# Scores of the next round moved into the visit of updates, values and reads: a recurrence and FFN kernel with a rewritten start

## The chip, the cores and the metric

The kernel runs on one core of a Trainium2 chip. The metric is the device time of one execution in microseconds (us); the time of a version is the median of several executions. PE is TensorE (its weight loads are listed apart, as PEld), DVE is VectorE, ACT is ScalarE, POOL is GpSimd, and SP is the engine whose queue issues all the DMAs here.

## The reference, cut to what matters

A linear recurrence with decay (4 batches, 8 heads, 768 positions, head size 32, state size 16) is followed by a feed-forward layer on its output (3072 tokens, 256 to 2048 to 256, softplus between).

```python
log_a = np.log(np.clip(a, 1e-06, 1.0))
for c in range(nc):                                  # chunks of 32 positions
    cum = np.cumsum(la, axis=-1)
    L = np.exp(cum[:, :, :, None] - cum[:, :, None, :]) * causal
    M = np.einsum('bhin,bhjn->bhij', Cc, Bc) * L
    y_intra = np.einsum('bhij,bhjd->bhid', M, xc)
    y_inter = np.einsum('bhin,bhnd->bhid', Cc, state) * np.exp(cum)[..., None]
    y[:, :, sl] = y_intra + y_inter
    state = decay_full * state + np.sum(Bx, axis=2)
h = x @ w_in                                         # x is y, by token
out = (np.maximum(h, 0.0) + np.log1p(np.exp(-np.abs(h)))) @ w_out
```

## The kernel before, in words

The 768 positions are cut into 6 rounds u of 128. A round of the recurrence gives the 512 tokens (4 batches x 128 positions) on which the feed-forward layer then works as block j = u.

In the recurrence a round has two halves p (two batches each). For each half the **scores** (word `S u.p`, tiles sp0 to sp3, line 379) are 16 matmuls that contract only 32 rows, four at a time side by side on a quarter of PE's rows. POOL makes the **decays** (`D`, tile rm, line 352) with a masked select from the factors fc; DVE **weighs** the scores with them (`M`, line 394). Then come the **updates** of the state (`U`, tile zp), the **values** (`I`, tiles yp) and the **reads** of the old state (`R`, also yp), all small matmuls on parts of PE; DVE makes the next state (`N`), multiplies the values by the growth factors (`G`), and the sum is split into a high and a low part (`Xh` on ACT, `Xl` on DVE).

The feed-forward layer is done in 128 x 512 matmuls. For each of 16 slices k of the 2048 inner columns there are 6 matmuls hp (`F`: high and low parts, lines 586 to 606), the softplus and its split on ACT and DVE (`P`, tiles e, gh, gl), and 6 matmuls acc (`Z`, lines 626 to 661). The weights come as 64-bit numbers in sixteen pieces (`w`), and are split into high and low parts in six stages each on ACT and DVE (`W`, line 543).

At the start logs of the decays are taken (`loga`, `logr`) and summed by matmuls with triangular **sum matrices** kc that are made on chip (line 162), which gives the factors by token (`ft`: tiles fp and total, then exp) and by row (`fr`: tiles sums and rp, then exp). Before that a few matmuls on zeros (`warm`) keep PE busy.

Three things set the order. Up to step 42 all engines follow a list of words written out by hand (ORDER, line 58), and PE follows the written order everywhere. After ORDER a step s runs one `Z` and one `F` (12 big matmuls), and the words of a round u from 3 on are put in at steps counted from the round's begin (FILLS, line 85); the other engines' instructions are then placed by a scheduler. And every tile in PSUM that is not an accumulator comes from a ring of 6 banks (tag ps): scores take 4 of them, a visit's zp and yp take 3, each hp takes 1.

```python
FILLS = (
    (-16, "D@.0 un@+.0 un@+.1 gg@+"),
    (-11, "S@.0 M@.0.0 M@.0.1 M@.0.2 M@.0.3 D@.1"),
    (-9, "C@ B@.0 B@.1 T@"),
    (-8, "S@.1 M@.1.0 M@.1.1 M@.1.2 M@.1.3"),
    (-5, "U@ I@.0 I@.1 R@ G@.0 G@.1 Xh@.0 Xh@.1 Xl@.0 Xl@.1 N@"),
)
```

In the profile most instructions have line 131 (135 in the changed kernel): it is the helper that puts an operation into the written order. They are told apart by their tiles. In what follows a *visit* is a stretch in which PE leaves the 128 x 512 matmuls for small ones and comes back.

Of the kernel before, what the change touches and what calls it, by code (L numbers as in the profile page):

```python
# [21 lines left out]
P = 128  # L22
# [17 lines left out]
TOKEN_GROUPS = ((0, 3), (3, 6))  # L40
ROW_GROUPS = ((1, 3), (3, 6))
# [11 lines left out]
C_MID = C_OWN + 3 * NB * (NC + 1)  # L53
# [30 lines left out]
RM = 2  # L84
FILLS = (
    (-16, "D@.0 un@+.0 un@+.1 gg@+"),
    (-11, "S@.0 M@.0.0 M@.0.1 M@.0.2 M@.0.3 D@.1"),
    (-9, "C@ B@.0 B@.1 T@"),
    (-8, "S@.1 M@.1.0 M@.1.1 M@.1.2 M@.1.3"),
    (-5, "U@ I@.0 I@.1 R@ G@.0 G@.1 Xh@.0 Xh@.1 Xl@.0 Xl@.1 N@"),  # L90
)

def constants():
# [7 lines left out]
    unit = np.arange(3 * NB * (NC + 1)) // (NC + 1)  # L101
# [9 lines left out]
def recurrence_then_ffn(ctx: ExitStack, tc: tile.TileContext, un, alr, w_in, w_out, const, outT):  # L111
# [31 lines left out]
    NL = S * NB * NH // P  # L143
    NR = NB * NH
# [705 lines left out]
```

## Time and profile before

| what | value |
|---|---|
| time, median of 3 runs | 315.08 us (314.93 to 315.32) |
| the profiled execution: its own time | 316.49 us |
| its span, first to last instruction | 314.8 us |
| mean granted TensorE clock | 0.999 |
| PE busy | 310.1 us (99%), 2315 matmuls |
| PE weight loads busy | 253.5 us (81%) |
| DVE / ACT / POOL busy | 158.3 / 169.0 / 38.0 us |
| HBM read, written | 20.76 MB, 3.24 MB |

The profiled execution took 1.41 us longer than the median of the timed runs. Matmuls overlap in the records (one starts while the one before it drains), so that a busy PE is read by the distance between starts and not by the length of a matmul. "x32" in a row stands for 32 instructions in a row that are alike.

### The profile page before, as it was taken

What the parts mean: (1) busy time and instruction counts of PE and PEld (TensorE: products, weight loads), DVE (VectorE), ACT (ScalarE), POOL (GpSimd) and SP (SyncE); (2) the same over time, 40 slices, a digit from 0 to 9 for tenths busy, and PEclk for the clock granted to TensorE, in tenths of its full rate; (3) what the DMA queues carried; (4) which work ended last, traced back from release to release, by engine and by line L of the source; (5) the groups of instructions that cost most, each with busy time, mean ns of one, the idle gap of its engine ahead of it and who ended that gap; (6) DMA issues with size and microseconds to landing.
All of it is one profiled execution on the core that took longest, in us unless ns stands there. A gap on an engine that the chain in (4) does not pass through costs nothing.

```text
span 314.8 us, 5625 instructions
## 1 busy us (share of the span) xinstructions
PE 310.1 (99%) x2315; PEld 253.5 (81%) x2315; DVE 158.3 (50%) x254; ACT 169.0 (54%) x290; POOL 38.0 (12%) x47
## 2 busy tenths in 40 slices
PE   8999999999999999999999999999999999999995
PEld 5887788888888878888888888888888888888885
DVE  3989995635744553454933254552344342322222
ACT  5789899788636364343344534344534344634450
POOL 5760900000000500000600000500000000000000
PEclk9999999999999999999999999999999999999999
DMA  7956956504000351000520100000100000100001
GB/s 242 401 216 207 374 188 159 175 1 167 2 0 0 117 199 55 34 3 0 202 70 0 67 2 0 3 2 0 67 3 0 3 0 0 69 0 0 2 0 67
DMA packets 10298, 24.37 MB, mean 77 GB/s; under 512 B 1056, under 2 KB 1696, under 8 KB 10272
## 3 DMA queue, kind: packets, MB, share of 16 engines
q1 hardware_dynamic: 10272, 24.01, 22.1%
q8 instruction: 18, 0.29, 0.4%
q14 instruction: 8, 0.07, 0.1%
HBM read 20.76 MB, written 3.24 MB: 76 GB/s over the span
## 4 chain that ended last, share of the span: by engine, by line
PE 98%; issue 0%; DVE 0%; POOL 0%; DVEq 0%; POOLq 0%
PE hp L131 42%; PE acc L131 41%; PE yp L131 5%; PE sp L131 5%; PE warm L131 1%; PE gp L131 1%; PE fp L131 1%; PE end L131 1%; PE zp L131 1%; DVE rm L131 0%; PE total L131 0%; PE rp L131 0%; DVE o_end L131 0%; PE sums L131 0%; POOL some L131 0%
## 5 line engine op out<-in xcount | busy, mean ns | idle before, releaser
L617 DVE TENSOR_TENSOR gl<-e,gh 128x512 fp32r<-128x512 f32 x54 | 37.3, 692 | 88.7 <-ACT gh L614 88.7
L131 PE MATMUL hp<-xh,wih 128*128 128x512 f32 (+1 forms) x196 | 76.2, 389 | 0.2 <-DVE rm L131 0.2
L131 PE MATMUL hp<-xl,wih 128*128 128x512 f32 (+1 forms) x196 | 75.6, 386 | 0.0
L131 PE MATMUL hp<-xh,wil 128*128 128x512 f32 (+1 forms) x196 | 75.5, 385 | 0.0
L131 PE MATMUL acc<-gh,woh 128*128 128x512 f32 x188 | 74.4, 396 | 0.0
L611 ACT ACTIVATE e<-hp 128x512 f32<-128x512 f32 x54 | 32.3, 598 | 76.8 <-PE hp L131 76.5
L131 PE MATMUL acc<-gl,woh 128*128 128x512 f32 x188 | 73.5, 391 | 0.0
L131 PE MATMUL acc<-gh,wol 128*128 128x512 f32 x188 | 73.2, 389 | 0.0
L131 DVE TENSOR_TENSOR gl<-e,gh 128x512 fp32r<-128x512 f32 x42 | 29.3, 707 | 33.2 <-ACT gh L131 33.1
L131 PEld LDWEIGHTS hp<-xh,wih 128*128 128x128 f32 x196 | 36.8, 188 | 8.6 <-DVE rm L131 1.1
L131 PEld LDWEIGHTS hp<-xh,wil 128*128 128x128 f32 x196 | 36.8, 188 | 7.7 <-DVE wil L131 0.4
L131 PEld LDWEIGHTS hp<-xl,wih 128*128 128x128 f32 x196 | 36.8, 188 | 7.2
L131 PEld LDWEIGHTS acc<-gh,woh 128*128 128x128 f32 x188 | 35.3, 188 | 8.6 <-issue 0.9
L131 PEld LDWEIGHTS acc<-gh,wol 128*128 128x128 f32 x188 | 35.3, 188 | 7.4
L131 PEld LDWEIGHTS acc<-gl,woh 128*128 128x128 f32 x188 | 35.3, 188 | 7.4 <-DVE gl L131 0.3
L131 ACT ACTIVATE e<-hp 128x512 f32<-128x512 f32 x42 | 24.5, 594 | 23.5 <-PE hp L131 19.7
L614 ACT CAST gh<-e 128x512 fp32r<-128x512 f32 x54 | 33.5, 620 | 4.1 <-PE acc L131 2.4
L131 POOL TENSOR_SCALAR_AFFINE_SELECT rm<-fc 128x512 f32<-128x512 f32 (+1 forms) x26 | 24.7, 985 | 81.1 <-PE yp L131 77.4
L131 ACT CAST gh<-e 128x512 fp32r<-128x512 f32 x42 | 25.3, 616 | 10.8 <-PE acc L131 10.4
L131 ACT ACTIVATE signs<-wraw 128x512 f16<-128x512 f32 (+1 forms) x32 | 24.2, 782 | 0.0
L131 DVE TENSOR_TENSOR rm<-sp,rm 128x512 f32<-128x512 f32 x32 | 20.4, 682 | 7.1 <-PE sp L131 6.8
L356 POOL TENSOR_SCALAR_AFFINE_SELECT rm<-fc 128x2048 f32<-128x2048 f32 x4 | 10.5, 2641 | 84.4 <-PE yp L131 84.4
(93 smaller groups left out, 219.7 us busy)
## 6 DMA issues: line engine op xcount, KB each, us to landing
un<-in_un SPq DMA_DIRECT2D x10, 768.0 KB, 6.2
wraw<-in_w_in SPq DMA_DIRECT2D x8, 512.0 KB, 5.1
wraw<-in_w_out SPq DMA_DIRECT2D x8, 512.0 KB, 4.3
gg<-gd SPq DMA_DIRECT2D x20, 128.0 KB, 3.5
out_t<-o SPq DMA_DIRECT2D x9, 256.0 KB, 2.1
head_in_h<-in_un SPq DMA_DIRECT2D x2, 384.0 KB, 5.1
head_in_l<-in_un SPq DMA_DIRECT2D x2, 384.0 KB, 6.7
out_t<-half SPq DMA_DIRECT2D x2, 256.0 KB, 2.2
```

Of the source, the lines that this page charges most:

```text
L131: return lambda *a, **k: tc.keep_in_program_order(f(*a, **k))
L356: Pl.affine_select(out=weights_of(u, p)[:, ks].rearrange("p h (c i) -> p (h c) i", i=SUB), in_=fs.rearrange("p h c -> p (h c)").unsqueeze( ...
L611: A.activation(e, h, AF.Softplus)
L614: A.copy(gh, e)
L617: V.tensor_tensor(gl, e, gh.bitcast(F32), op=ALU.subtract)
```

## The change

The scores of a round's first half leave their own visit and stand behind the reads of the round before (`S@+.0` in the line of FILLS at -5; `S3.0` behind `R2` in ORDER); the scores of the second half keep a visit of their own. To have the decays that early, `D` of the first half is moved up by about a round, and for rounds 3 and 5 its tiles lie in the room of the raw weights (AHEAD_OF_TIME), in two pieces each. The logs come in two DMAs, first those of rounds 0 and 5 with the copy for the growth, then the others, and both groups of factors are cut accordingly. The sum matrices come from one select on POOL and seven small DVE operations. The zeros that `warm` writes are one tile, and there are eight such matmuls ahead of the first useful one and two further on. One half of the values of round 0 is put into an accumulator's bank. Two memsets go from DVE to POOL. ORDER is another list; of its 300 or so words the diff shows the first row only.

```diff
-TOKEN_GROUPS = ((0, 3), (3, 6))
-ROW_GROUPS = ((1, 3), (3, 6))
+NR = NB * NH
+LAST = NU - 1
+ROW_GROUPS = ((1, LAST), (LAST, NU))
...
-C_MID = C_OWN + 3 * NB * (NC + 1)
+C_MID = C_OWN + (LAST - 1) * NB * (NC + 1)
...
-la warm7 loga loga ft0 logr us0.0 w0 logr gb ft0 kb S0.0 ux0.0 W0 growth gq0 us0.1 growth ux0.1 D0.0.0 W0 M0.0.0 ft0 D0.0.1
...
+la warm6 warm1 kb loga lb warm1 loga logr logb fr1 fr1 logr us0.0 growth ft0 gb ft0 ft0 w0 ft0 ft0 D0.0.2 growth S0.0
...
+AHEAD_OF_TIME = ((3, 0), (5, 0))
 FILLS = (
-    (-16, "D@.0 un@+.0 un@+.1 gg@+"),
-    (-11, "S@.0 M@.0.0 M@.0.1 M@.0.2 M@.0.3 D@.1"),
+    (-16, "D@.1 un@+.0 un@+.1 gg@+"),
+    (-14, "D@+.0"),
+    (-11, "S@.1 M@.1.0 M@.1.1 M@.1.2 M@.1.3"),
     (-9, "C@ B@.0 B@.1 T@"),
-    (-8, "S@.1 M@.1.0 M@.1.1 M@.1.2 M@.1.3"),
-    (-5, "U@ I@.0 I@.1 R@ G@.0 G@.1 Xh@.0 Xh@.1 Xl@.0 Xl@.1 N@"),
+    (-5, "U@ I@.0 I@.1 R@ S@+.0 G@.0 G@.1 N@ Xh@.0 Xh@.1 Xl@.0 Xl@.1"),
+    (-4, "M@+.0.0 M@+.0.1 M@+.0.2 M@+.0.3"),
 )
...
-    both_logs = cp.tile([P, NA + NR + NL], F32, name="both_logs")
-    la, lr = both_logs[:, : NA + NR], both_logs[:, NA + NR :]
+    first_logs = cp.tile([P, 3 * NR], F32, name="first_logs")
+    other_logs = cp.tile([P, NA - 2 * NR + NL], F32, name="other_logs")
+    lo, lr = other_logs[:, : NA - 2 * NR], other_logs[:, NA - 2 * NR :]
-    level = cp.tile([P, 2], F32, name="level")
+    level = cp.tile([P, 1], F32, name="level")
...
-        Pl.memset(level[:, :1], 1.0)
-        Pl.memset(level[:, 1:], 0.5)
-        V.memset(kc, 0.0)
-
-        def below(rows, at, n, value, fill):
-            Pl.affine_select(
-                out=kc[rows, at : at + n],
-                in_=value[rows].broadcast_to([rows.stop - rows.start, n]),
-                pattern=[[-1, n]],
-                compare_op=ALU.is_gt,
-                fill=fill,
-                base=rows.start,
-                channel_multiplier=1,
-            )
-
+        Pl.memset(level, 1.0)
+        V.memset(kc[:, : NC * P], 0.0)
+        later = kc[:, NC * P :]
+        Pl.affine_select(
+            out=later,
+            in_=level.broadcast_to([P, P]),
+            pattern=[[-1, P]],
+            compare_op=ALU.is_gt,
+            fill=0.0,
+            base=0,
+            channel_multiplier=1,
+        )
         for c in range(NC):
             n = SUB * (c + 1)
+            own = slice(SUB * c, n)
             if c:
-                below(slice(0, SUB * c), c * P, n, level[:, :1], 0.0)
-            below(slice(SUB * c, n), c * P, n, level[:, 1:], -0.5)
-        below(slice(0, P), NC * P, P, level[:, :1], 0.0)
+                V.tensor_copy(kc[: SUB * c, c * P : c * P + n], later[: SUB * c, :n])
+            V.tensor_scalar(kc[own, c * P : c * P + n], later[own, :n], 1.0, -0.5, op0=ALU.mult, op1=ALU.add)
...
+    zeros = []
+
     def warm(n):
-        w = pa.tile([P, 512], F32, tag="acc0", name=f"warm{n}")
+        if not zeros:
+            zeros.append(pa.tile([P, 512], F32, tag="acc0", name="zeros"))
         for _ in range(n):
             PE.matmul(
-                w[:32].rearrange("p (a b) -> p a b", b=32),
+                zeros[0][:32].rearrange("p (a b) -> p a b", b=32),
...
-        u0, u1 = TOKEN_GROUPS[g]
-        n = (u1 - u0) * NR
-        la_g = la[:, u0 * NR : u1 * NR]
+        us = (0, LAST) if g == 0 else range(1, LAST)
+        logs = first_logs[:, : 2 * NR] if g == 0 else lo
+        n = len(us) * NR
         fp = ps.tile([P, 512], F32, tag="ps", name=f"fp{g}")
         for i in range(NC):
-            PE.matmul(fp[:, i * n : (i + 1) * n], kc[:, i * P : (i + 1) * P], la_g, start=True, stop=True)
+            PE.matmul(fp[:, i * n : (i + 1) * n], kc[:, i * P : (i + 1) * P], logs, start=True, stop=True)
         yield
         by_chunk = fp[:, : NC * n].rearrange("p (c k) -> p c k", c=NC)
-        for v0, v1 in ((u0, 1), (1, u1)) if u0 == 0 else ((u0, u1),):
-            cols, at = slice(v0 * NR, v1 * NR), slice((v0 - u0) * NR, (v1 - u0) * NR)
-            A.activation(fc[:, cols].rearrange("p k c -> p c k"), by_chunk[:, :, at], AF.Exp)
+        runs = ((0, 1), (LAST, NU)) if g == 0 else ((1, LAST),)
+        total, at = None, 0
+        for u0, u1 in runs:
+            here, cols = slice(at, at + (u1 - u0) * NR), slice(u0 * NR, u1 * NR)
+            at = here.stop
+            A.activation(fc[:, cols].rearrange("p k c -> p c k"), by_chunk[:, :, here], AF.Exp)
             yield
-            if v0 == u0:
+            if total is None:
                 total = ps.tile([P, 512], F32, tag="ps", name=f"total{g}")[:, :n]
-                PE.matmul(total, kc[:, NC * P : K_END], la_g, start=True, stop=True)
+                PE.matmul(total, kc[:, NC * P : K_END], logs, start=True, stop=True)
                 yield
-            A.activation(ft[:, cols], total[:, at], AF.Exp)
+            A.activation(ft[:, cols], total[:, here], AF.Exp)
             yield
 
     def factors_by_row(g):
         u0, u1 = ROW_GROUPS[g]
+        logs = lo if g == 0 else first_logs[:, NR : 2 * NR]
         n, nu = (u1 - u0) * NR, (u1 - u0) * NB
         sums = ps.tile([P, 512], F32, tag="ps", name=f"sums{g}")[:n, : NC + 1]
-        PE.matmul(sums, la[:, u0 * NR : u1 * NR], kb[:, C_MID:C_END], start=True, stop=True)
-        yield
-        by_head = p2.tile([P, 3 * NB, NC + 1], F32, tag="by_head", name=f"by_head{g}", bufs=1)[:n, :nu]
+        PE.matmul(sums, logs, kb[:, C_MID:C_END], start=True, stop=True)
...
-    def weights_of(u, p):
+    def weights_of(u, p, k0, k1):
+        if (u, p) in AHEAD_OF_TIME:
+            half = k0 * 2 // KP
+            if ("m", p, half) not in mid[u]:
+                t = p3.tile([P, 512, 2], I32, tag="wraw", name=f"rm{u}_{p}{half}", bufs=WRAW)
+                mid[u]["m", p, half] = t.rearrange("p f t -> p (f t)").bitcast(F32).rearrange("p (h t) -> p h t", t=P)
+            return mid[u]["m", p, half][:, k0 - half * KP // 2 : k1 - half * KP // 2]
         if ("m", p) not in mid[u]:
             mid[u]["m", p] = p3.tile([P, KP, P], F32, tag="rm", name=f"rm{u}_{p}", bufs=RM)
-        return mid[u]["m", p]
+        return mid[u]["m", p][:, k0:k1]
 
     def decays(u, p, k=None):
-        ks = slice(0, KP) if k is None else slice(k * KP // 4, (k + 1) * KP // 4)
+        if k is None:
+            n = KP // 2 if (u, p) in AHEAD_OF_TIME else KP
+            for k in range(0, KP, n):
+                decays_of(u, p, slice(k, k + n))
+        else:
+            decays_of(u, p, slice(k * KP // 4, (k + 1) * KP // 4))
...
-            mid[u]["yp"] = [ps.tile([P, 512], F32, tag="ps", name=f"yp{u}_{k}") for k in range(2)]
+            mid[u]["yp"] = [
+                pa.tile([P, 512], F32, tag="acc1", name="yp0_0")
+                if u == k == 0
+                else ps.tile([P, 512], F32, tag="ps", name=f"yp{u}_{k}")
+                for k in range(2)
+            ]
...
-            V.memset(t, 0)
+            Pl.memset(t, 0)
...
-        "la": lambda: load(both_logs, alr),
+        "la": lambda: load(first_logs, alr[:, : 3 * NR]),
+        "lb": lambda: load(other_logs, alr[:, 3 * NR :]),
...
-        "loga": staged(lambda: log_clipped(la)),
+        "loga": staged(lambda: log_clipped(first_logs)),
+        "logb": staged(lambda: log_clipped(lo)),
...
-                if u < NU - 1 or w[0] not in "BTUNug":
+                if u < NU - 1 or w[0] not in "BTUN" and "+" not in w:
...
-        "alr": c(np.concatenate([la, lg, lr], 1)),
+        "alr": c(np.concatenate([la[:, :NR], la[:, LAST * NR :], lg, la[:, NR : LAST * NR], lr], 1)),
```

On PE, at round 3's visit (yp3 are its values and reads, cc3 and tb3 what the reads take, sp4 the scores of round 4, acc the big matmuls that follow), the rows of before are

```order
L131 MATMUL yp3_0_1709<-cc3_1583,tb3_1340 64x128 x2
L131 MATMUL yp3_1_1710<-cc3_1583,tb3_1340 64x128 x2
L131 MATMUL acc0_2_1492<-gh2_8_1607,woh1_854 128x512
L131 MATMUL acc0_2_1492<-gl2_8_1609,woh1_854 128x512
L131 MATMUL acc0_2_1492<-gh2_8_1607,wol1_855 128x512
L131 MATMUL acc1_2_1493<-gh2_8_1607,woh1_854 128x512
```

and of the change

```order
L135 MATMUL yp3_0_1713<-cc3_1611,tb3_1314 64x128 x2
L135 MATMUL yp3_1_1714<-cc3_1611,tb3_1314 64x128 x2
L135 MATMUL sp4_00_1763<-un4_1436 128x128
L135 MATMUL sp4_01_1764<-un4_1436 128x128
L135 MATMUL sp4_02_1765<-un4_1436 128x128
L135 MATMUL sp4_03_1766<-un4_1436 128x128
```

The 16 scores of round 4's first half (12 more rows like the last four) now stand between the reads and acc; before, they had a place of their own between two hp and acc groups.

On PE at the start of the program, where warm and zeros are the matmuls on zeros, fp and total lead to the factors by token, sums to those by row (it reads the constants kb), and sp0 are the first scores, the rows of before are

```order
L131 LDWEIGHTS some_88
L131 MATMUL warm7_118<-some_88 32x512
L131 MATMUL fp0_128<-both_logs_73,kc_76 128x96 x4
L131 MATMUL sp0_00_142<-head_in_h_85 128x128
L131 MATMUL sp0_01_143<-head_in_h_85 128x128
```

and of the change

```order
L135 LDWEIGHTS some_89
L135 MATMUL zeros_110<-some_89 32x512
L135 MATMUL sums1_125<-kb_78,first_logs_73 32x5
L135 MATMUL fp0_132<-first_logs_73,kc_77 128x64 x4
L135 MATMUL total0_140<-first_logs_73,kc_77 128x64
L135 MATMUL sp0_00_149<-head_in_h_86 128x128
```

The sums have moved ahead of fp, total ahead of the scores, and the last matmul on zeros is the eighth and not the seventh.

On POOL behind that, where rm0 and rm1 are the decays of rounds 0 and 1 (then the half), four selects of 128 x 512 to a half, the rows of before are

```order
L131 AFFINE_SELECT rm0_0_175<-fc_89 128x512 x4
L131 AFFINE_SELECT rm0_1_188<-fc_89 128x512
L131 AFFINE_SELECT rm1_0_214<-fc_89 128x512
L131 AFFINE_SELECT rm0_1_188<-fc_89 128x512 x3
L131 AFFINE_SELECT rm1_0_214<-fc_89 128x512
```

and of the change

```order
L135 AFFINE_SELECT rm0_0_146<-fc_90 128x512 x4
L135 AFFINE_SELECT rm0_1_203<-fc_90 128x512 x2
L135 AFFINE_SELECT rm1_0_263<-fc_90 128x512
L135 AFFINE_SELECT rm0_1_203<-fc_90 128x512 x2
L135 AFFINE_SELECT rm1_0_263<-fc_90 128x512
```

Two selects of round 0's second half stand behind the first one of round 1, which reads factors of the other group; before, these were three, and rounds 0 to 2 had their factors from one group.

## Rows read from the trace of the kernel before

**Rows 1.** Page, part 2: granted TensorE clock in 40 slices.
```profile
PEclk9999999999999999999999999999999999999999
```
**Rows 2.** Windows: busy time per engine in a stretch, PEclk, DMA share, GB/s.
```profile
40.00:300.00 260.00, 260.00 (x1749) 213.40 (x1749) 121.71 (x193) 133.34 (x228) 15.35 (x6) 1.00 0.14 47
```
**Rows 3.** Timeline, PE: scores alone (start, length, engine, line, operation).
```profile
179.03 0.39 PE L131 MATMUL hp<-xl,wih 128*128 128x512 f32 x1
179.25 0.39 PE L131 MATMUL hp<-xh,wil 128*128 128x512 f32 x1
179.57 1.17 PE L131 MATMUL sp<-un 32*128 32x128 f32 x32
180.68 0.50 PE L131 MATMUL acc<-gh,woh 128*128 128x512 f32 x1
181.01 0.40 PE L131 MATMUL acc<-gl,woh 128*128 128x512 f32 x1
```
**Rows 4.** Timeline, PE: inside a visit, updates to values, values to reads.
```profile
149.03 0.41 PE L131 MATMUL zp<-un,bp 128*32 128x64 f32 x16
149.26 0.29 PE L131 MATMUL yp<-rm,un 128*32 128x128 f32 x3
...
150.89 0.29 PE L131 MATMUL yp<-rm,un 128*32 128x128 f32 x4
151.12 0.33 PE L131 MATMUL yp<-cc,tb 32*64 32x128 f32 x3
```
**Rows 5.** Timeline, PE: the start, up to the first updates of round 1.
```profile
0.98 3.17 PE L131 MATMUL warm<-some 128*32 128x512 bf16 x7 [0.98 <-POOL some L131]
...
4.08 2.02 PE L131 MATMUL fp<-both_logs,kc 128*128 128x96 f32 x8
...
6.03 2.09 PE L131 MATMUL sp<-head_in_h 32*128 32x128 f32 x32
...
10.50 1.10 PE L131 MATMUL yp<-rm,head_in_h 128*32 128x128 f32 x32
...
13.22 1.16 PE L131 MATMUL gp<-kc,logs 128*128 128x128 f32 x8
...
15.71 1.08 PE L131 MATMUL yp<-rm,head_in_l 128*32 128x128 f32 x32
...
16.72 0.71 PE L131 MATMUL sp<-un 32*128 32x128 f32 x13
...
18.80 0.36 PE L131 MATMUL hp<-xh,wih 128*128 128x256 f32 x1
...
29.54 0.65 PE L131 MATMUL zp<-un,bp 128*32 128x64 f32 x32
```
**Rows 6.** Timeline, the other engines and DMA issues at the start.
```profile
1.74 2.46 POOL L131 TENSOR_SCALAR_AFFINE_SELECT kc<-level 32x32 f32<-32x32 f32 x8 [0.75 <-DVE kc L131]
...
2.17 0.47 SPq L140 DMA_DIRECT2D kb<-in_const  x1
...
6.61 3.44 POOL L131 TENSOR_SCALAR_AFFINE_SELECT rm<-fc 128x512 f32<-128x512 f32 x5 [2.04 <-ACT fc L131]
...
8.21 2.48 DVE L131 TENSOR_TENSOR rm<-sp,rm 128x512 f32<-128x512 f32 x4 [2.66 <-PE sp L131]
...
11.32 0.41 DVE L131 TENSOR_TENSOR bp<-head_in_h,ft 128x256 f32<-128x256 f32 x1
...
15.47 0.92 ACT L131 ACTIVATE fc<-fp 128x384 f32<-128x384 f32 x1 [0.46 <-PE fp L131]
...
20.61 0.92 DVE L131 TENSOR_TENSOR bp<-un,ft 128x256 f32<-128x256 f32 x1
```
**Rows 7.** DMA issues: name, queue, count, KB, median us to landing.
```profile
both_logs<-in_alr SPq DMA_DIRECT2D x1, 208.0 KB, 2.4
kb<-in_const SPq DMA_DIRECT2D x1, 97.5 KB, 5.2
```
**Rows 8.** Timeline, PE: a big matmul that waited for a free bank.
```profile
38.80 0.50 PE L131 MATMUL hp<-xh,wih 128*128 128x512 f32 x1 [0.19 <-DVE rm L131]
```

More of the change, by code (lines that the diff above doesn't have):

```diff
@@ new lines @@
+D0.1.2 W2 W2 gq0 D0.1.1 W0 gq0 W2 I0.0 B0.1 un1.0 ft1 G0.0 S0.1 M0.1.1 M0.1.2 D1.0.3 fr1 gd W0 w1 W2 gq1 D0.1.0 ft1 w4
+M0.1.0 D0.1.3 M0.1.3 fr0 fr0 U0 Xh0.0 warm1 gq1 I0.1 D1.0.2 D1.1.1 D1.0.1 ft1 tl w5 warm1 S1.0 Xl0.0 W0 W1 D1.1.3
+un1.1 D1.0.0 G0.1 W2 H1 Xh0.1 N0 W1 Xl0.1 M1.0.2 M1.0.3 W4 W1 D1.1.2 H0 B1.0 M1.0.1 W4 w3 F0.0 P0.0 P0.0 F0.3 W4 F0.1
+D1.1.0 M1.0.0 B1.1 W1 P0.3 P0.0 W4 W1 F0.2 S1.1 W1 W4 P0.1 P0.1 W4 Z0.0 M1.1.2 gg1 M1.1.1 M1.1.0 P0.2 P0.2 w6 W6 W3
+un2.0 W6 P0.2 F0.4 F0.5 P0.1 C1 W6 W6 W3 P0.3 W6 M1.1.3 Z0.1 U1 I1.0 w7 W3 W6 W3 W3 W3 I1.1 gg3 W5 P0.4 R1 G1.1 G1.0
@@ new lines @@
+w13 W11 F0.9 Z1.6 P0.11 W14 W11 W14 P0.12 Z1.7 W11 P0.8 P0.8 W14 K1.0 P0.10 W14 S2.0 K1.1 P0.12 W13 w15 W13 W15 P0.9
+M2.0.0 W15 P0.10 P0.10 Z0.8 F0.15 M2.0.2 F1.15 P0.9 W15 F0.14 F0.13 P0.15 P0.12 P0.9 W13 F1.10 W13 P0.14 Z0.9 Z0.10
+W13 W13 P0.15 W15 P0.15 Z0.11 P0.13 W15 W15 P0.14 P0.14 M2.0.1 P0.13 C2 P0.13 D3.0.2 Z0.12 P1.10 F1.8 F1.9 P1.8 P1.15
+Z0.13 P1.15 Z0.14 Z0.15 P1.10 P1.10 P1.9 D2.1.1 D2.1.0 P1.8 P1.8 P1.9 E0 F1.13 D2.0.3 P1.13 F1.11 S2.1 P1.9 B2.1
+M2.1.1 D2.1.2 M2.1.3 M2.1.2 M2.1.0 M2.0.3 Z1.8 Z1.9 U2 I2.0 I2.1 P1.13 P1.11 N2 P1.11 R2 S3.0 P1.13 G2.1 D3.0.1 G2.0
@@ L77 @@
+D3.0.0 Xh2.0 M3.0.0 D3.0.3 P1.11 Xh2.1 Z1.10 M3.0.1 F1.12 P1.12 F1.14 Xl2.0 P1.12 P1.14 Z1.11 Xl2.1 P1.15 P1.14 M3.0.3
+M3.0.2 P1.12 P1.14
 """
@@ L209, in spread_logs @@
         A.activation(
-            t.rearrange("p (k d) -> p k d", d=D), la[:, NA:].unsqueeze(2).broadcast_to([P, NR, D]), AF.Copy
+            t.rearrange("p (k d) -> p k d", d=D),
+            first_logs[:, 2 * NR :].unsqueeze(2).broadcast_to([P, NR, D]),
+            AF.Copy,
         )
@@ L308, in factors_by_row @@
         u0, u1 = ROW_GROUPS[g]
+        logs = lo if g == 0 else first_logs[:, NR : 2 * NR]
         n, nu = (u1 - u0) * NR, (u1 - u0) * NB
         sums = ps.tile([P, 512], F32, tag="ps", name=f"sums{g}")[:n, : NC + 1]
-        PE.matmul(sums, la[:, u0 * NR : u1 * NR], kb[:, C_MID:C_END], start=True, stop=True)
+        PE.matmul(sums, logs, kb[:, C_MID:C_END], start=True, stop=True)
         yield
-        by_head = p2.tile([P, 3 * NB, NC + 1], F32, tag="by_head", name=f"by_head{g}", bufs=1)[:n, :nu]
+        by_head = p2.tile([P, (LAST - 1) * NB, NC + 1], F32, tag="by_head", name=f"by_head{g}", bufs=1)[:n, :nu]
         V.tensor_tensor(
@@ L356, in decays @@
         Pl.affine_select(
-            out=weights_of(u, p)[:, ks].rearrange("p h (c i) -> p (h c) i", i=SUB),
+            out=weights_of(u, p, ks.start, ks.stop).rearrange("p h (c i) -> p (h c) i", i=SUB),
             in_=fs.rearrange("p h c -> p (h c)").unsqueeze(2).broadcast_to([P, n * NC, SUB]),
@@ L488, in within @@
                         home(u, p)[:, U_X + k * D : U_X + (k + 1) * D],
-                        m[:, k],
+                        weights_of(u, p, k, k + 1)[:, 0],
                         start=fresh(u, bank, [hh]),
```

43 lines of the change are left out of this document (9 added, 34 removed).

## The prediction

> **What bounds the kernel now.** I read the windows by stage first. From 40 to 300 us PE is busy for 260.00 of 260.00 us at a granted clock of 1.00 [rows 2], while DVE has 122 and ACT 133: nothing but PE's own sequence of matmuls sets the time there, and a microsecond is saved only by fewer or cheaper steps on PE. Then I read the timeline of PE by the distance between starts. Two big matmuls in a row start 0.22 to 0.23 us apart (179.03, 179.25) [rows 3]; I call 0.23 a step. What a visit costs beyond its own small matmuls shows at its edges: from the last hp to the first score 0.32 us pass instead of a step, and from the first acc to the second 0.33 [rows 3], so 0.09 or 0.10 on the way in and 0.10 or 0.11 on the way out. The page's clock row is 9 throughout [rows 1]. Yet the first 32 scores take 2.09 us [rows 5] and later ones of the same shape 1.17 [rows 3]: the start runs as if at the lower of the clock's two levels (1.2 of 2.4 GHz), though the record grants the upper one, and the trace doesn't name the moment at which this ends. Last I read the start on all engines: there PE waits for others and the others for PE.
>
> **The three joined visits.** On PE the scores of the first half of rounds 3, 4 and 5 move from visits of their own to the end of a visit that is made anyway. The scores themselves stay (32 records in 180.68 - 179.57 = 1.11 us). One way in and one way out go: 0.09 + 0.11 = 0.2 each, 0.21 with the unrounded starts of such rows, times 3: **-0.6 us**.
>
> What the trace does not show is the seam from the reads (form 32*64) to the scores (form 32*128). Two rows bound it. Updates and values have the same form, 128*32, and there the last 16 updates take 149.26 - 149.03 = 0.23 us, 0.06 for four, with no pause. Values to reads change the form, and the last four values hold 151.12 - 150.89 = 0.23 us where four take 1.86 / 16 = 0.12 on average (151.12 - 149.26 for 64) [rows 4]: a pause of about 0.11. I take the pause, since this seam changes the form too; such a pause at the end of the reads and another at the begin of the scores were paid in the separate visits as well, so that -0.6 already holds them. If the seam were free like the first one, both would go, 0.11 + 0.11 each time, and the three visits would give -0.6 - 0.66 = -1.3.
>
> The Trainium skill (TensorEngine Tiling (Array Packing), Key Properties) says that changing the tiling mode, and not just the tile, drains TensorE, and its list of modes has 32x128 and 32x64 as different ones. By it the seam pauses and the joint visit gives -0.6; by the free seam it would be -1.3. The values-to-reads row agrees with it, 0.23 us instead of 0.12; for this very seam no row of before exists.
>
> **What hides the rest of that move.** A joint visit needs 3 + 4 banks of a ring of 6. The fourth score tile takes the bank of zp, which DVE frees with `N`, now placed right behind. Between zp and the scores lie the values and reads, some 2.9 us (1.86 for the values, about 1 for the reads), and `N` is two short DVE operations: cost nothing. If `N` were late, PE would stand still. Next on DVE come two `G`, two `C`, two `Xl` and the first `M` before the first bank of the scores is free: at about 0.62 us each (2.48 for 4 [rows 6]) 7 x 0.62 = 4.4 us behind the reads, and one or two gl beside them. The third hp after the visit takes that bank, and it starts five groups of six steps behind the scores, 1.1 + 5 x 1.38 = 8.0 us behind the reads. Cost nothing; bound: one wait per visit like the one in [rows 8]. The decays that are moved up need free tiles and POOL time. POOL works for 15 of the 260 us [rows 2], and six more instructions' overhead is hidden there.
>
> **The start, where PE's work moves.** (a) The eighth matmul on zeros adds 3.1 / 7 = 0.44 us, and two sums of five columns ahead of fp some 0.25 (an estimate): fp starts at 4.08 + 0.69 = 4.8. (b) fp keeps its eight records (their length goes by the weights, I take the same 1.95 us, 6.03 - 4.08), and total, some 0.4 at this clock, now precedes the scores: these start at 7.1 instead of 6.03 [rows 5]. (c) `M` of the first half starts 8.21 - 6.03 = 2.2 behind them, at 9.3, and takes 2.48 [rows 6], to 11.8; POOL's selects start 0.7 late and end before that. So the first values come at 12.0 instead of 10.50. (d) But PE does in the gap what it did later. In before 18.80 - 10.50 = 8.30 us lie between the first values and the first hp. Of these go: sums, fp and rp between gp (from 13.22, 1.0 long) and the values at 15.71, 1.5 us, and the waiting among the scores at 16.72, 18.80 - 16.72 - 1.11 - 0.24 for a total = 0.7 [rows 5]. An rp (0.3) and two more matmuls on zeros (0.43) come in. 8.3 - 1.5 - 0.7 + 0.7 = 6.8: the first hp at 18.8. (e) POOL now has a select of round 1 ahead of two of round 0. It waits for ACT's exp of the other group's fp, 512 columns, 0.92 x 512 / 384 = 1.2 us [rows 6], behind an exp of gp (gp ends just ahead of the values, at 12.0, and 0.6 for it); so 13.8, three selects of 3.44 / 5 = 0.69 to 15.9, one `M`, 16.6: the second values, due at 16.5, wait some 0.3 in their middle. First hp at **19.1 to 19.2, 0.35 later than before**.
>
> (f) From there to the first updates of round 1 before takes 29.54 - 18.80 = 10.74 us [rows 5] for 24 half-width and 24 full steps (36 x 0.23 = 8.3), a score visit (1.3) and an rp (0.3): 0.8 of it is waiting. In the change rp and total are done, and 12 acc matmuls are put in ahead, which are only moved. So 19.15 + 8.3 + 1.3 = 28.75 plus new waits, against 29.54. For these: POOL's selects of round 1 now run all through the splitting of x and of the weights on DVE, and a DVE operation beside POOL can take 0.92 instead of 0.41 (bp at 20.61 and 11.32 [rows 6]). Bounds: none, or as much waiting as before, 0.8. I take half, 0.4, since the parts that hp waits for (xl, wil) come out within some tenths of the time at which they are due. The start gives 28.75 + 0.4 - 29.54 = **-0.3 to -0.4; I take -0.3**, between -0.8 and +0.1.
>
> **After the start.** The scores of round 2 no longer follow the visit of round 1 at once. In before a big matmul behind them waited for a bank that DVE held, 0.19 us idle and 0.1 to get going [rows 8]: **-0.3**, if no new wait comes; bounds -0.5 and +0.3.
>
> **Edits that cost nothing.** The sum matrices: eight selects kept POOL until 4.20 [rows 6]; now one select and seven DVE operations on at most 128 columns end well before the matmuls on zeros do, at 4.4. If that cover went, each tenth would delay fp. Two memsets on POOL, the bank for a half of values, the split of the logs (one more DMA issue, 0.4 us of SP) lie beside the same matmuls. The second DMA of logs brings 160 KB, which 208 KB in 2.4 us [rows 7] puts at about 4; ACT needs them at 8.
>
> **Sum.** -0.6 - 0.3 - 0.3 = -1.2 us. The profiled execution took 316.49, so 315.3 for the changed one; it stood 1.41 above the median, and the median of 315.08 becomes 313.9, of which I say **313.8** with the unrounded edges.
>
> **Rivals.** *A free seam*: -0.7 more, 313.1. For it: all these forms use 32 rows. Against: every change of form in rows 3 and 4 pauses. 12 in 100. *The start gives back what the visits give*: waits of 0.8 and more before the first updates of round 1, or the low clock level staying longer, so that gp, fp and sums take up to twice their time; the start then gives +0.4 instead of -0.3, 314.5. For it: ACT and POOL have more in front of the second values than before. Against: POOL has room in front, it waited 2.04 there [rows 6]. 18 in 100. *A wait per joint visit takes the place of the pauses*: 0.2 + 0.1 to 0.4 us each as in [rows 8], three times, and one more at round 2, so +1.2: 315.0, no change. 8 in 100. *Slower*: the sums at the head of PE's queue need the constants kb, and fp and all else is queued behind them. In before kb landed 5.2 us after its issue [rows 7]. Issued second (about 1.2), it would land at 6.4, PE would be free at 4.4, and the whole start comes 2.0 us later: 315.8. It costs from a landing after 4.4 on and makes the kernel slower from one at about 6.3. Against: it was the fourth load, behind 208 KB that alone took 2.4 us [rows 7] and two larger ones; now only the first logs' 48 KB stand before it. 8 in 100. That the scores don't join the visit is excluded by PE's order.
>
> **How the numbers follow.** The forecast holds 54 in 100. Its own bounds: -1.3 - 0.8 - 0.5 on one side, +0.1 and +0.3 on the other. The range 312.7 to 315.1 takes in the free seam, the poorer start and the wait per visit, and leaves out kb. About 0.2% (0.6 us) is what a measurement of this kernel can tell from no change. Faster by more (below 314.45): the forecast but for a few of its cases, the free seam and a part of the poorer start, 0.71. Same: the rest of it and the waits, 0.19. Slower (above 315.7): 0.10.
>
> **What would show it.** In the changed profile: three scores that start right behind reads, with about 0.2 us from the last four reads to the first score and no idle time; no score visits before the updates of rounds 3 to 5 but the second halves'. fp at 4.8, first values near 12.0, the first hp at 19.1, the updates of round 1 near 31.9 (with 12 acc ahead of them). PE busy for all of the time from 40 us on. It would be wrong if the first sums start after 4.6, if hp idles behind a joint visit, or if the first hp comes after 20.

## The result, and the profile after

The changed kernel takes **318.12 us** (median of 4 executions, 317.60 to 319.30) where the kernel before took 315.02 beside it: ratio 1.0102, 95% interval 1.0072 to 1.0132. It is 3.1 us slower; 313.8 was forecast, with a range of 312.7 to 315.1. The profiled execution took 319.3 us with a span of 317.6, before 316.49 and 314.8; the 2.8 us between the spans are what the traces have to explain.

The start [rows 5] now, from PE's timeline:

```profile
0.98 3.59 PE L135 MATMUL zeros<-some 128*32 128x512 bf16 x8 [0.98 <-POOL level L135]
4.36 0.27 PE L135 MATMUL sums<-kb,first_logs 128*32 128x5 f32 x2
4.56 1.97 PE L135 MATMUL fp<-first_logs,kc 128*128 128x64 f32 x8
...
6.89 2.09 PE L135 MATMUL sp<-head_in_h 32*128 32x128 f32 x32
9.14 2.08 PE L135 MATMUL fp<-other_logs,kc 128*128 128x128 f32 x8
...
11.29 1.81 PE L135 MATMUL gp<-kc,logs 128*128 128x128 f32 x8
13.03 1.08 PE L135 MATMUL yp<-rm,head_in_h 128*32 128x128 f32 x32
...
15.15 1.16 PE L135 MATMUL gp<-kc,logs 128*128 128x128 f32 x8
...
19.75 0.38 PE L135 MATMUL hp<-xh,wih 128*128 128x256 f32 x1
...
32.51 0.65 PE L135 MATMUL zp<-un,bp 128*32 128x64 f32 x32
```

The sums start at 4.36, so kb is not late. The first values come at 13.03, the first hp at 19.75 and the updates of round 1 at 32.51, with 12 acc now ahead of them. Twelve big matmuls in a row take 2.72 us in the kernel before (the chain below), so like for like it is 29.79, against 29.54: in this pair of executions the start is 0.25 us longer. (In before these 12 acc stood behind a visit, from 32.90 to 35.84; those 2.94 us hold the edges of visits as well, and the edges remain.)

A joined visit, and its like in the kernel before (second fence), both on PE's timeline:

```profile
150.22 0.65 PE L135 MATMUL zp<-un,bp 128*32 128x64 f32 x32
150.69 1.93 PE L135 MATMUL yp<-rm,un 128*32 128x128 f32 x64
152.55 1.10 PE L135 MATMUL yp<-cc,tb 32*64 32x128 f32 x32
153.59 1.17 PE L135 MATMUL sp<-un 32*128 32x128 f32 x32
154.69 0.51 PE L135 MATMUL acc<-gh,woh 128*128 128x512 f32 x1
```
```profile
198.54 0.65 PE L131 MATMUL zp<-un,bp 128*32 128x64 f32 x32
199.02 1.93 PE L131 MATMUL yp<-rm,un 128*32 128x128 f32 x64
200.88 1.10 PE L131 MATMUL yp<-cc,tb 32*64 32x128 f32 x32
201.91 0.50 PE L131 MATMUL acc<-gh,woh 128*128 128x512 f32 x1
```

The visit grows from 3.37 to 4.47 us; a visit of scores alone cost 0.09 + 1.11 + 0.10 = 1.30 [rows 3]. The reads last 1.04 ahead of scores and 1.03 ahead of a big matmul, so this seam pauses like the other. The last four reads alone, ahead of the first score at 153.59:

```profile
153.37 0.29 PE L135 MATMUL yp<-cc,tb 32*64 32x128 f32 x4
```

They hold 0.22 us, where the 28 before them take 0.12 for four. About 0.2 is saved per joined visit, as forecast.

What was not forecast shows at three places. **First, all the way along**: the end of the chain of waits (start, length, engine, tile), of before and then of after.

```profile
274.64 2.72 PE acc L131 x12
305.92 2.80 PE acc L131 x12
308.72 2.87 PE end L131 x24
```
```profile
276.69 2.75 PE acc L135 x12
308.28 2.80 PE acc L135 x12
311.08 2.84 PE end L135 x24
```

Twelve big matmuls take 2.75 us instead of 2.72. Between the two acc rows lie 138 steps: 31.28 us before, 31.59 after, 226.67 and 228.91 ns a step. The same difference stands in the stretches from 40 us on, for hp and acc alike, while the granted clock is 1.00 in both. There are 1128 such matmuls.

**Second, a stand of PE** behind the joined visit of round 2. The window of 40 to 300 us (its columns as in [rows 2], where PE was busy for all of it) lacks 0.84 us of PE, which the prediction's signs had as busy throughout:

```profile
40.00:300.00 260.00, 259.16 (x1765) 211.47 (x1764) 120.30 (x192) 132.19 (x224) 20.75 (x14) 1.00 0.14 47
```

The timelines of PE, DVE and ACT at the place:

```profile
113.34 0.39 PE L135 MATMUL acc<-gh,woh 128*128 128x512 f32 x1
...
114.71 0.40 PE L135 MATMUL acc<-gh,woh 128*128 128x512 f32 x1
115.95 0.50 PE L135 MATMUL acc<-gl,woh 128*128 128x512 f32 x1 [0.84 <-DVE gl L135]
116.29 0.40 PE L135 MATMUL acc<-gh,wol 128*128 128x512 f32 x1
...
117.22 0.39 PE L135 MATMUL hp<-xh,wih 128*128 128x512 f32 x1
```
```profile
113.42 0.68 DVE L135 TENSOR_TENSOR gl<-e,gh 128x512 fp32r<-128x512 f32 x1
114.02 1.28 DVE L135 TENSOR_TENSOR rm<-sp,rm 128x512 f32<-128x512 f32 x2
115.22 1.28 DVE L135 TENSOR_TENSOR gl<-e,gh 128x512 fp32r<-128x512 f32 x2
```
```profile
112.80 0.62 ACT L135 CAST gh<-e 128x512 fp32r<-128x512 f32 x1
```

From 114.71 to 115.95 is 1.24 where a step is 0.23, and the next step takes 0.34: 1.1 lost. The gl that acc wants (slice 12 of block 1) could have been made from 113.42 on, when ACT's gh was ready; but ORDER has the gl of slice 15 and two weighings of the moved scores ahead of it on DVE.

**Third, the end**: from PE's end to the end of the span 314.8 - 311.59 = 3.2 us before, 317.6 - 313.92 = 3.7 after.

The bank wait of [rows 8] is gone. Its worth is read by starts too, from the matmuls around it in the kernel before:

```profile
38.21 0.39 PE L131 MATMUL hp<-xh,wil 128*128 128x512 f32 x1
...
39.13 0.40 PE L131 MATMUL hp<-xl,wih 128*128 128x512 f32 x1
```

With the row at 38.80 between them it is 0.59 - 0.23 = 0.36, and 0.33 - 0.23 = 0.10 for the step behind: 0.46.

The balance from the updates of round 1 to the end: 314.8 - 29.54 - 2.72 = 282.5 before, 317.6 - 32.51 = 285.1 after. That is +2.6 = longer steps 2.1 (shown below) + stand 1.1 + end 0.5 - three joined visits 0.6 - the bank wait 0.5. The 0.25 of the start make up the 2.8 of the spans.

### The profile page after: what moved, and what is told of

The parts are those of the page before. It is cut to its first block, busy times and chain, and to the rows that moved or that the text cites. A ratio compares the mean times of both kernels' runs of the same rounds, so it can differ in the third digit from the quotient of the medians.

```text
span 317.6 us, 5643 instructions
## 1 busy us (share of the span) xinstructions
PE 312.1 (98%) x2318; PEld 255.2 (80%) x2318; DVE 155.8 (49%) x260; ACT 169.4 (53%) x291; POOL 38.6 (12%) x45
## 4 chain that ended last, share of the span: by engine, by line
PE 96%; DVE 2%; issue 1%; POOL 0%; DVEq 0%; POOLq 0%
PE hp L135 41%; PE acc L135 40%; PE yp L135 5%; PE sp L135 4%; PE fp L135 1%; PE zeros L135 1%; PE zp L135 1%; PE end L135 1%; PE gp L135 1%; DVE rm L135 1%; DVE gl L135 0%; DVE xl L135 0%; PE total L135 0%; DVE o_end L135 0%; PE rp L135 0%
## 5 line engine op out<-in xcount | busy, mean ns | idle before, releaser
L631 DVE TENSOR_TENSOR gl<-e,gh 128x512 fp32r<-128x512 f32 x54 | 37.3, 692 | 93.6 <-ACT gh L628 93.6
L625 ACT ACTIVATE e<-hp 128x512 f32<-128x512 f32 x54 | 32.3, 599 | 78.9 <-PE hp L135 78.6
L135 DVE TENSOR_TENSOR gl<-e,gh 128x512 fp32r<-128x512 f32 x42 | 30.9, 746 | 28.8 <-ACT gh L135 28.7
L135 POOL TENSOR_SCALAR_AFFINE_SELECT rm<-fc 128x512 f32<-128x512 f32 (+1 forms) x30 | 29.1, 1004 | 78.2 <-ACT signs L135 39.2
L135 ACT ACTIVATE signs<-wraw 128x512 f16<-128x512 f32 (+1 forms) x32 | 23.5, 783 | 0.0
L379 POOL TENSOR_SCALAR_AFFINE_SELECT rm<-fc 128x1024 f32<-128x1024 f32 (+1 forms) x4 | 7.6, 1910 | 87.0 <-PE yp L135 70.6
```

The costliest lines, as they stand in the source:

```text
L135: return lambda *a, **k: tc.keep_in_program_order(f(*a, **k))
L379: Pl.affine_select(out=weights_of(u, p, ks.start, ks.stop).rearrange("p h (c i) -> p (h c) i", i=SUB), in_=fs.rearrange("p h c -> p (h c)" ...
L625: A.activation(e, h, AF.Softplus)
L631: V.tensor_tensor(gl, e, gh.bitcast(F32), op=ALU.subtract)
```

## Experiments on the longer step

No instruction of the hp and acc matmuls changed, so the theory was their place in SBUF. The larger kb (215 columns for 195) moves the weight tiles (wih, wil, wo) by 64 bytes, the larger by_head (4 rounds' room for 3) moves x, gh and gl by 64 more. Each of these kernels only adds unused bytes, and e8 also has the order of e4 below. In the table, places are the first bytes of wih and of xh modulo 256 in the built programs (wo and gh stand to each other alike), *distance* is their difference modulo 256, and the step is the mean over the 138 steps.

| kernel | padding | wih | xh | distance | step, ns | median, us (before beside it) |
|---|---|---|---|---|---|---|
| before | | 64 | 64 | 0 | 226.67 | |
| changed | | 128 | 192 | 64 | 228.91 | 318.12 (315.02) |
| e1, from before | 64 behind by_head | 64 | 128 | 64 | 228.91 | 317.63 (315.12) |
| e2, from changed | apart + 64 | 128 | 0 | 128 | 232.46 | 321.94 (315.12) |
| e3, from changed | 192 behind kb, apart + 192 | 64 | 64 | 0 | 226.67 | 317.30 (315.12) |
| e6, from before | 32 ahead of level | 96 | 96 | 0 | 226.67 | 315.28 (315.36) |
| e8, from changed, reordered | 64 behind kb, apart + 64 | 192 | 64 | 128 | 233.33 | 321.80 (315.36) |
| e9, from changed | apart + 192 | 128 | 128 | 0 | 226.67 | 315.97 (315.49) |
| e10, from changed | apart + 128 | 128 | 64 | 192 | 233.33 | 323.05 (315.49) |
| e13, from before | 32 behind by_head | 64 | 96 | 32 | 233.41 | 322.32 (315.20) |
| e14, from before | 224 behind by_head | 64 | 32 | 224 | 233.33 | 322.64 (315.20) |

The edits: e9 (e2 has 24 columns, e10 40); the second line of e3 (its first is that of e9; e8 has 16 and 24 columns, and the order of e4 below); e6; and e1 (16), e13 (8), e14 (56).

```diff
-    cp.tile([P, 8], F32, name="apart")
+    cp.tile([P, 56], F32, name="apart")
```
```diff
+    cp.tile([P, 48], F32, name="apart_too")
     level = cp.tile([P, 1], F32, name="level")
```
```diff
+    cp.tile([P, 8], F32, name="apart_too")
     level = cp.tile([P, 2], F32, name="level")
```
```diff
-        by_head = p2.tile([P, 3 * NB, NC + 1], F32, tag="by_head", name=f"by_head{g}", bufs=1)[:n, :nu]
+        by_head = p2.tile([P, 3 * NB * (NC + 1) + 16], F32, tag="by_head", name=f"by_head{g}", bufs=1)[:n, : nu * (NC + 1)]
+        by_head = by_head.rearrange("p (u c) -> p u c", c=NC + 1)
```

*e1.* 

> The kernel before with 64 bytes of padding behind by_head, so that all tiles behind it (x in two parts, gh, gl, e, rm, un) lie 64 bytes further and no weight tile moves; not one instruction changes. Placement theory (the step of a big matmul depends on where its weights and its moving operand lie in SBUF; in the changed kernel the weight tiles moved by 64 bytes and x, gh, gl by 128, so that their distance changed by 64): the step goes from 226.7 to about 229 ns here too, 1128 steps x 2.3 ns = 2.6 us, so 317.5. Rival (the longer step comes from the new order or the new traffic of POOL and DVE, or from the execution): step 226.7, 315.0.

*e2.* 

> The changed kernel with the unused tile apart of 24 columns instead of 8: x, gh, gl and the rest behind it lie 64 bytes further, the weights stay, the order of all instructions stays. If the distance between weights and moving operand (modulo 128 bytes) counts, it is again that of before: step 226.7, 318.1 - 2.5 = 315.6. If each operand's own place counts (weights or x off their old place modulo 128): step 229 or longer, 318 or more. If placement does not count: 318.1 with the step as in the changed kernel.

*e3.* 

> The changed kernel with 192 bytes of padding behind kb and 192 more in apart: weights at 256 bytes from their place in before, x, gh, gl at 512, both the same as before modulo 256; order unchanged. Placement theory: step 226.7 and 315.6, and the scatter between executions falls to that of before. Rival (order, POOL and DVE traffic, execution): 318.1, step 229.

The end of e1's chain of waits:

```profile
274.91 2.75 PE acc L131 x12
306.50 2.80 PE acc L131 x12
```

31.59 us lie between them, as in the changed kernel. So e1 shows that the place of tiles is the cause: the old kernel with 64 bytes more and the same instructions has the step of the changed one and is slower by 0.8% (interval 0.5 to 1.0). e3 gets the old step back in the changed order. Its median missed the 315.6, and its scatter did not fall to that of before: seven of ten executions took 317.1 to 317.4, the others 315.3 to 316.3, the profiled one, with the old step, 316.1. What the seven did differently no trace shows; that it is the start (below) is a guess. The first reading of e2 rested on a slip of mine: the pad does not bring the distance back but makes it 128. The step, 232.5, fitted the other reading, own places, at that time.

*e6.* 

> The kernel before with 32 bytes of padding ahead of level: weights and moving operands all lie 32 bytes further, no instruction changes. So far weights or moving operand at 0 modulo 128 cost 2.25 ns each per step, at 64 nothing. If only starts at a multiple of 128 cost: step 226.7, 315.1. If a start off a multiple of 64 costs as well: step 229 to 231, 317.5 to 320.

*e8.* 

> As the kernel with both repairs, but with 64 bytes of padding behind kb and 64 more in apart: weights at 192, x, gh and gl at 64 modulo 256, both at 64 modulo 128 as in before. If the place modulo 128 is what counts: step 226.7 and the same time as with the other padding. If modulo 256: step about 229, 2.5 more.

e6 leaves the step alone with both operands moved by 32. e8 refutes my reading of that time (each operand's own place modulo 128: both stand at 64 there, and the step is the worst). Set beside each other, the seven kernels so far have one order: the distance.

*e9.* 

> The changed kernel with apart of 56 columns instead of 8, nothing else: weights stay at 128 modulo 256 (0 modulo 128), x, gh, gl come to 128 modulo 256. Distance theory (the step depends on the place of the moving operand less that of the weights, modulo 256 bytes: 0 in the kernel before, 64 in the changed one, 128 where it was 231 to 233): the distance is a multiple of 256 again, step 226.7, 315.6 to 317.3 as with both paddings. Rival (each operand's own place counts: both at 0 modulo 128): step 231 or more, 321.

*e10.* 

> The changed kernel with apart of 40 columns: distance 192 modulo 256. If what counts is how near the two streams are, in either direction (192 is 64 short of 256): step 229, 318. If the cost grows with the distance (0, 64, 128: 226.7, 229, 231 to 233): 234 or more, 323. By own places (weights at 0, x at 64 modulo 128, as in the changed kernel): 229, 318.

e9 was the decisive one: both operands off their old places, but a multiple of 256 apart. The end of its chain of waits, and that of e10 below it:

```profile
272.96 2.72 PE acc L135 x12
304.24 2.80 PE acc L135 x12
307.04 2.87 PE end L135 x24
```
```profile
278.74 2.80 PE acc L135 x12
310.94 2.80 PE acc L135 x12
```

31.28 us for the 138 steps, as in before, and 32.20 in e10, whose step refutes the reading that 192 is as near as 64. From the updates of round 1 on e9 takes 313.6 - 30.65 = 282.95 where the changed kernel took 285.1: the longer step cost 2.1 us of that stretch.

*e13.* 

> The kernel before with 32 bytes of padding behind by_head: distance 32 modulo 256 between moving operand and weights, no instruction changed. If the cost grows evenly with the distance (64: 2.3 ns, 128: 4.4 to 6.6, 192: 6.7): step 227.8, 316.6. If it goes in jumps of 64: 226.7 or 228.9. Rival (0 is not the lowest point): below 226.7, faster than before.

*e14.* 

> The same with 224 bytes: distance 224 modulo 256. If the cost grows with the distance up to a jump back at 256: step 233.3 or more, 323. If it falls again towards 256: below 233. If in jumps of 64: 233.3.

None of e13's three readings came. The cost is no slope, and it doesn't go in jumps of 64: 32 costs as much as 192, 6.7 ns a step, and 64 a third of it. Of the distances tried only 0 is free, and none is below it; the kernel before stood on the best one, by luck of its tile sizes. The distance isn't the whole of it: e2 and e8 have the same one, and their steps differ by 0.9 ns.

The pads move tiles of ACT and DVE as well. The window of e10 without a visit (columns as in [rows 2]) tells against a collision of theirs with PE:

```profile
280.00:300.00 20.00, 20.00 (x87) 16.15 (x86) 4.85 (x7) 8.15 (x14) 0.00 (x0) 1.00 0.00 0
```

DVE works for 4.85 of the 20 us and ACT for 8.15, yet every single step there is longer than before, 230 to 236 ns between starts against 226 to 227.

## Experiments on the other terms

*e4*, the changed kernel with gl 12 first, in ORDER (words of two lines, joined):

```diff
-Xl2.1 P1.15 P1.14 M3.0.3 M3.0.2 P1.12 P1.14
+Xl2.1 P1.12 P1.15 P1.14 M3.0.3 M3.0.2 P1.14
```

> The changed kernel with the last stage of P1.12 (gl of round 1, part 12, on DVE) ahead of gl 15 and of the two last weighings of round 3's first half, instead of behind them. Theory (the stand of 1.0 us of PE at 114.9 is gl 12 queued behind two weighings on DVE): the stand goes, 318.1 - 1.0 = 317.1, step unchanged. Rival (the ring of four gh holds PE up anyway: gh 14 comes at 115.0 behind an acc): gl 14 is then late instead, and less than 0.4 is won.

Measured: 317.57 beside 315.12, ratio 1.0080 (1.0060 to 1.0100). The 12 acc at this place, in the chain of waits:

```profile
113.06 2.75 PE acc L135 x12
```

In the changed kernel 117.22 - 113.34 = 3.88 us pass from the first of them to the hp behind them. The wait is gone, so the theory held in the trace: from the updates of round 1 to the end 315.9 - 32.05 = 283.85, which is 1.2 less than 285.1. The median fell by 0.55 only, and the two intervals overlap.

*e5*, e3 and e4 together:

> Both repairs together: the changed kernel with its tiles back at their place modulo 256 and with gl 12 ahead of the weighings. If both are separate terms: step 226.7, no stand at 113 to 115, PE's work from round 1's updates to its end shorter than in before by the joined visits (0.65) and the bank wait (0.3); 317.3 - 1.1 = 316.2 median, 314.2 to 316.3 over the executions, about 1 above what the prediction made of the whole change at most, because the start has not become shorter. Rival: the repaired order brings another stand later; 317.

Measured: 315.16 beside 315.36, ratio 0.9998 (0.9981 to 1.0014), better than expected by 1.0. DVE's row at the place of the stand, where both gl now precede the weighings:

```profile
111.42 1.29 DVE L135 TENSOR_TENSOR gl<-e,gh 128x512 fp32r<-128x512 f32 x2
112.62 1.28 DVE L135 TENSOR_TENSOR rm<-sp,rm 128x512 f32<-128x512 f32 x2
```

From the updates on it takes 312.8 - 30.85 = 281.95, against 282.5 in before: the joined visits and the bank wait, 1.1, less the end's 0.5.

*e11*, e5 and four small instructions more on POOL:

```diff
+        for k in range(4):
+            Pl.memset(spare[:, k : k + 1], 0.0)
```

> The version with both repairs and four more one-column memsets on POOL at the start. Between PE's last matmul and the end of the span lie 3.7 us in all versions of the changed order and 3.2 in before and in the joined visits alone; 0.42 of it is a gap in front of POOL's second closing semaphore. Theory (the gap hangs on where POOL's closing instructions stand in its own program: 74 records with the gap, 77 and 82 without): the tail falls to 3.2 and the median to 315.2 - 0.4 = 314.7. Rival (it comes from SP's five waits instead of four or the new order): 3.7, 315.2.

Measured: 314.64 beside 315.49, ratio 0.9985 (0.9969 to 1.0001). The last chain row and the span give 312.8 - 309.51 = 3.3: the 0.4 of the end is gone.

```profile
306.64 2.87 PE end L135 x24
```

From the updates on: 312.8 - 31.45 = 281.35, or 1.15 less than before. That four memsets do it is shown (e12, which has them too, ends like e11; all eight other profiles of the new order have 3.6 to 3.7); that it is a matter of where POOL's closing instructions lie is only argued.

*e7*, the kernel before with the joined visits that hold the scores of rounds 4 and 5 alone: AHEAD_OF_TIME and FILLS of the change, but for u = 3 a table that keeps the old words for round 3's own scores.

```diff
+FILLS_OF_3 = (
+    (-16, "D@.0 un@+.0 un@+.1 gg@+"),
+    (-14, "D@+.0"),
+    (-11, "S@.0 M@.0.0 M@.0.1 M@.0.2 M@.0.3 D@.1"),
...
+    (-8, "S@.1 M@.1.0 M@.1.1 M@.1.2 M@.1.3"),
...
-        for at, words in FILLS:
+        for at, words in FILLS_OF_3 if u == 3 else FILLS:
```

> The kernel before with the joined visits of rounds 4 and 5 alone (the scores of their first half behind the reads of the round before, decays ahead of time in the wraw buffers); start, order up to step 32, sum matrices, logs and placement as in before. By the prediction: no pause beyond the two at the seams, 0.22 less per joined visit, 0.43 in all, 314.7, step 226.7. Free seam: 0.43 + 2 x 0.22, 314.2. Rival (a wait per joint visit, hp for a bank of the scores): 315.1 or more, with the wait in the timeline.

Measured: 314.51 beside 315.36, ratio 0.9982 (0.9972 to 0.9992), the only version here that is surely faster than before. Its visit takes 4.47 us as above and no big matmul behind it waits:

```profile
197.49 0.65 PE L142 MATMUL zp<-un,bp 128*32 128x64 f32 x32
...
200.86 1.17 PE L142 MATMUL sp<-un 32*128 32x128 f32 x32
201.96 0.50 PE L142 MATMUL acc<-gh,woh 128*128 128x512 f32 x1
202.29 0.40 PE L142 MATMUL acc<-gl,woh 128*128 128x512 f32 x1
```

From the updates of round 1 on: 313.5 - 28.69 = 284.8, where before takes 314.8 - 29.54 = 285.3; 0.4 less, and two visits at 0.2 were expected.

*e12*, e11 with three matmuls on zeros more, in ORDER:

```diff
-D0.0.2 growth S0.0
+D0.0.2 growth warm3 S0.0
```

> The same with three more matmuls on zeros ahead of the first scores. In executions in which the first scores run at the higher level PE waits there for the rows of head_in (0.3 to 1.3 us), so three fillers of 0.2 cost 0 to 0.4; where they run at the lower level they cost 1.3 us, unless the denser work brings the higher level earlier than 10 to 13 us. If it does: the scatter between executions shrinks and the median falls by some 0.3. Rival: no change of the moment, 0.3 to 1.0 us slower.

Measured: 314.91 beside 315.49, ratio 0.9992 (0.9975 to 1.0008), 0.3 above e11, executions from 313.97 to 316.19 where e11's went from 313.85 to 315.80. The scatter did not shrink: no gain shown, the rival is nearer.

**The start in the profiles.** The moment at which PE comes to the upper level of its clock, read from the lengths of like matmuls, differs between profiles of one order. Where the first scores take 1.2 us it rose between 4 and 6 us, where they take 2.1 later. In e9 (PE timeline):

```profile
6.28 1.17 PE L135 MATMUL sp<-head_in_h 32*128 32x128 f32 x32
...
10.50 1.17 PE L135 MATMUL yp<-rm,head_in_h 128*32 128x128 f32 x32
...
18.05 0.39 PE L135 MATMUL hp<-xh,wih 128*128 128x256 f32 x1
...
30.65 0.65 PE L135 MATMUL zp<-un,bp 128*32 128x64 f32 x32
```

| profile | first scores take | level up by | first values | first hp | updates of round 1, 12 acc ahead |
|---|---|---|---|---|---|
| before [rows 5] | 2.09 | 10.5 | 10.50 | 18.80 | 29.54 + 2.72 = 32.26 |
| e11, new order | 2.09 | 10.9 | 11.93 | 18.86 | 31.45 |
| changed | 2.09 | 13.0 | 13.03 | 19.75 | 32.51 |
| e7, old order | 1.17 | 5.6 | 9.03 | 17.29 | 28.69 + 2.72 = 31.41 |
| e9, new order | 1.17 | 6.0 | 10.50 | 18.05 | 30.65 |
| e5, new order | 1.17 | 5.8 | 10.38 | 18.24 | 30.85 |

In this table, with the level up at about the same time, the new start is 0.6 to 0.8 us shorter than the old one; in the profiled execution of the changed kernel the level came 2.5 us later than in that of before, and the gain was gone. The other profiles take the gain away: early ones of the old order have 31.0 (e1) and of the new one 30.7 to 32.05 (e10, e2, e3, e4), late ones 32.1 to 32.3 in the old order (e6, e13, e14) and 32.95 in the new one (e8). Over all executions the new start costs time: e5's ratio says -0.1 us and its stretch behind the start -0.6, which leaves +0.5 for the start; in the same way +0.4 for e9, +0.7 for e11 and +0.6 for the changed kernel. These are estimates, each with the stretch of a single profile.

## Why the prediction was wrong

**The step that failed** is the first one: "I call 0.23 a step", taken for both kernels. The sum held only what is added, removed and moved on PE, and took the length of the 1128 matmuls that stay as given. The change made it 2.2 ns longer by moving their operands apart by 64 bytes, 2.1 us behind the start: almost twice the whole gain that was forecast. The edits that do it (a wider kb, a wider by_head) were not costed at all: "Edits that cost nothing" looks at instructions, not at where tiles come to lie.

**The work behind the joined visit of round 2** was sized too low. The prediction counted what DVE has in front of a bank (two `G`, two `C`, two `Xl`, an `M`, "one or two gl beside them") and saw no wait. Right for the bank: no hp waited for it. But the same queue makes the gl that acc needs, and there gl 12 stood behind two weighings: 1.1 us (1.2 by e4). The rival "a wait per joint visit" had the wrong tile and the wrong number: it is one wait of 1.1, only where the order is written by hand, and none behind the later visits.

**The joined visits**: -0.6 forecast, two of them measured at -0.4 (e7), so 0.6 for three. Right in size and mechanism, a pause at the new seam included; the free seam is out. This is where the Trainium skill (TensorEngine Tiling (Array Packing), Key Properties) was cited: that a change of tiling mode drains TensorE agrees with the 0.22 us, for 0.12, that the last four reads hold ahead of the scores.

**The bank wait** of [rows 8]: -0.3 forecast (0.19 idle and 0.1 to get going), 0.46 by starts. It isn't in every execution: the profiles of e1, e13 and e14, with the instructions of before, lack it.

**The start** failed too: -0.3 forecast, +0.25 in the profiled pair and some +0.5 over the executions (the estimates above). Steps (a) and (b) held nearly: sums at 4.36, fp at 4.56 for 4.8, scores at 6.89 for 7.1. Step (c) took the time of the first values from DVE, and DVE was ready:

```profile
9.07 2.48 DVE L135 TENSOR_TENSOR rm<-sp,rm 128x512 f32<-128x512 f32 x4 [3.37 <-PE sp L135]
```

The weighing ended at 11.55, but the values came at 13.03 and not at 12.0. What held them was PE's own queue, into which rp, fp, sums and gp had moved, at the lower level: fp took 2.08 us (1.16 in e9), gp 1.81 at 11.29 and 1.16 at 15.15. So the first hp of step (d) came at 19.75 instead of 19.15; from there to the updates 12.76 us, as forecast (31.9 - 19.15). The rival "The start gives back what the visits give" had named the low level, and it came about besides the longer step.

**The end**, 0.5, was in no step.

**The slower rival** (kb lands late) did not happen: the sums followed the matmuls on zeros at once. The kernel got slower by something that no rival named.

With the three side effects mended (e11: distance, gl 12 and end) the change is worth less than the 1.2 that was forecast: its ratio to before, 0.9985, is 0.5 us, with an interval from 1.0 faster to 0.03 slower. The stretch behind the start gains 1.15, and the start gives a part of it back.

## What to carry to other kernels

When a change adds or widens a tile, list the addresses of the operands of the dominant matmul before and after: here a distance between moving operand and weights that is a multiple of 256 bytes is worth up to 6.7 ns a step, 7 us of 315. If a uniform loss appears, divide a long stretch by its count of steps before looking for waits, and undo it with a pad before judging the change. When work is put into a visit, follow each engine's queue to the next consumer that PE has, not only to the buffer that the moved work itself takes.

## What the runs showed of the hardware

A 128x512 matmul's step goes by how far its moving operand lies from its weights in a partition: 226.67 ns at a distance of 0 modulo 256 bytes, 228.9 at 64, 232.5 and 233.3 at 128, 233.3 to 233.4 at 32, 192 and 224; moving both by 32 or 64 bytes changes nothing (e6, e9). Which access meets which is not shown. The Trainium skill (SBUF — State Buffer, A bandwidth-pool intuition that's wrong) gives TensorE's weight loads a second, independent read port. It says nothing of places; whoever takes from it that the place of the weights cannot count finds it otherwise here, and the measurement decides.

TensorE's level at the start is not in the granted clock: that is 1.00 from 0 to 16 us in both kernels, with PE busy for all of 2 to 16 us, while eight gp matmuls of the changed kernel take 1.81 us at 11.29 and 1.16 at 15.15, and the first scores of the old order 2.09 us in one profile and 1.17 in another (1.2 and 2.4 GHz). The Trainium skill (TensorE: Matmul & The Clock Gate, Seeing it yourself) warns that the clock gate's trace events have been unreliable, and these rows agree. Executions of one version differ by 1.5 us and more, and an effect of 0.3 us needs the stretch behind the start, not the whole time.

Four small memsets on POOL at the start took 0.4 us from the end of the kernel (3.7 to 3.3 us between PE's last matmul and the end of the span).
